# First token tiles one by one, and the value projection as TensorE's first work

## The chip, the cores and the metric

The kernel runs on one core of one Trainium2 chip. The metric is the time of one execution in device microseconds (us). Four runs of the kernel before gave 172.43 to 172.70 us, median 172.57 us. One execution was also recorded by the hardware profiler; "the trace" is its record, and times inside it count from the start of its span.

## The reference

For x of 2048 tokens by 448 features, in bf16:

```python
xn = layernorm(x)                                  # no weights, eps 1e-5
q, k, v = split(xn @ wqkv)                         # 16 heads of 28
# token s attends to s, s-2, ..., s-14 (8 keys, dilation 2), softmax over them
s = attention(q, k, v) @ wo
g = silu(gelu_tanh(xn @ w1 + b1) @ w2 + b2)        # 448 -> 1792 -> 448
out = x + s * g
```

## The kernel before

**Tokens.** Even and odd tokens are stored as two halves of 1024, so that a dilated window becomes 8 neighbours. There are 16 tiles of 128 tokens, in 4 chunks of 4 tiles. Attention is cut into blocks of 112 queries (128 at the start of a half), each of which needs 128 keys and values.

**Work of one chunk.** For each tile VectorE takes mean and variance (`stats`, L334: `bn_stats`, `bn_aggr`), ScalarE a square root and VectorE a reciprocal (`rstds`, L345), and VectorE writes the normalised tile (`norm`, L362). A row has 448 values; the 64 beyond 384 are written twice, so that the last part of the contraction can run in the upper or the lower half of TensorE's rows. In the first two chunks TensorE transposes the tile (L376) into a PSUM bank and ScalarE or VectorE copies it out into `xnT` (L380); in the last two a DMA transposes it. Then come the projections: query and key (`qk`, L417), value (`vproj`, L440), the first feed-forward matmul (`ff1`, L461, evacuated by a gelu on ScalarE with the bias `b1`), attention (`attn`), the second feed-forward matmul (`ff2`) and the output (`final`).

**Contractions in batches.** A contraction over 448 is three full matmuls of 128 rows and a tail of 64 rows. `batch` (L384) groups jobs: the closed jobs run their full matmuls first, then all tails run in pairs, one in each half of the array, then the opened jobs run their full matmuls. Each job holds one of 8 PSUM banks until ScalarE or VectorE has copied it out.

**Weights.** Query and key weights are loaded raw (`wraw`, and `wraw3` for the last 64 rows) and copied into a padded layout (`wqk`, `wqk3`, L320 to L329) by ScalarE or VectorE. Value weights (`wv`) and the feed-forward weights (`w1`, `w2`) are used as loaded.

**Who decides the order.** Each piece of work is a task with engines it may run on, an estimated cost, what it depends on, a priority and the buffers that it takes and gives. A list scheduler (`_Plan.run`, L73) goes through them and fixes one order for each engine's queue; the tasks are then written out in that order (L691). On the chip each engine works through its queue strictly in that order. So a changed cost or priority can move work anywhere in the kernel, and an instruction whose data is ready still waits behind an earlier one of its engine. Loads are issued by SyncE (SP) or ScalarE's queue in that order too.

**The start.** Up to 40 dummy matmuls on zeros (L272, "warm", while the plan's clock is under 12) keep TensorE busy until there is work. Tiles 0 and 1 are loaded from SP, 2 and 3 from ScalarE's queue (L313), then the raw query and key weights from SP. The square roots of tiles 0 and 1 are one instruction, those of 2 and 3 another (L603). All later loads except that of `b1` wait for the statistics of tile 0 (`t_hold`, L607, a small memset on VectorE); the value weights are issued from ScalarE's queue after the first square root (L608). The bias `b1` comes in as 14 rows, is transposed by TensorE (L626) and copied out by VectorE (L630, the tile is called `b` in the profile); every gelu needs it.

Of the kernel before, what the change touches and what calls it, by code (L numbers as in the profile page):

```python
# [10 lines left out]
ALU = mybir.AluOpType  # L11
ACT = mybir.ActivationFunctionType
# [131 lines left out]
def kernel(  # L144
# [12 lines left out]
    nc = tc.nc  # L157
    P = 128
    S, D, H, DH, F = A_x.shape[1], 448, 16, 28, 1792
# [5 lines left out]
    KF = 3 * P  # L165
# [3 lines left out]
    TPC = CH // P  # L169
# [15 lines left out]
    def rows(halves, pos, n):  # L185
        h, r = divmod(pos, HALF)
        return halves[h, r:r + n, :]
# [4 lines left out]
    def sb(name, shape, dt=BF16):  # L192
        return const.tile(shape, dt, name=name)
# [3 lines left out]
    x_sb = sb("x_sb", [P, NT, D])  # L197
# [4 lines left out]
    wv = sb("wv", [P, KT, D])  # L202
    w1 = sb("w1", [P, KT, F])
    w2 = sb("w2", [P, NMT, D])
    wo = sb("wo", [P, KT, D])
    b1r = sb("b1r", [NMT, P])
    b1 = sb("b1", [P, NMT], F32)
    b2 = sb("b2", [P, D])
# [9 lines left out]
    mv = sb("mv", [P, NT, 2], F32)  # L218
    sd = sb("sd", [P, NT], F32)
    rstd = sb("rstd", [P, NT], F32)  # L220

    def ring(name, n, shape, dt=BF16, fifo=False):
        return _Pool([sb(f"{name}{i}", shape, dt) for i in range(n)], fifo)

    p_xn = ring("xn", 6, [P, 512])
    p_st = ring("st", 4, [P, 6], F32)
# [14 lines left out]
    plan = _Plan()  # L241
# [7 lines left out]
    def act(n):  # L249
        return 0.19 + n / 1200.0  # L250

    def dve(n, r=1):
        return 0.15 + n / (960.0 * r)
# [10 lines left out]
    def memset(eng, ap, v):  # L264
        def fn(_):
            getattr(nc, eng).memset(ap, v)  # L266
        return fn
# [11 lines left out]
    def mk_ident(_):  # L279
# [5 lines left out]
    t_wz = [plan.add("DVE", 0.3, memset("vector", wqk[:, :, :, DH:], 0.0), [t_on], prio=98),  # L285
            plan.add("DVE", 0.1, memset("vector", wqk3[:, :, DH:], 0.0), [t_on], prio=97)]
# [3 lines left out]
    def dma(eng, dst, src, kb, prio, deps=()):  # L290
        def fn(_):
            (nc.sync if eng == "SP" else nc.scalar).dma_start(dst, src)  # L292
        a = plan.add(eng, 0.45, fn, [t_on] + list(deps), prio)
        return plan.add("DMA", kb / 310.0, lambda _: None, [a], prio, tail=1.7)
# [7 lines left out]
    t_x = {}  # L302

    def load_x(t0, n, prio, eng="SP", deps=()):
        d = dma(eng, x_sb[:, t0:t0 + n, :],
                rows(x_half, t0 * P, n * P).rearrange("(t p) d -> p t d", p=P), 112 * n, prio, deps)
        for t in range(t0, t0 + n):
            t_x[t] = d

    def ktiles(ap):  # L310
        return ap.rearrange("(k p) c -> p k c", p=P)

    for t in range(TPC):  # L313
        load_x(t, 1, 99 - t, "SP" if t < 2 else "ACT")
    t_raw = dma("SP", wraw[:], ktiles(A_wqkv[0:KF, 0:2 * D]), 672, 97)
    t_raw3 = [dma("SP", wraw3[64 * i:64 * i + 64, :], A_wqkv[KF:D, i * D:(i + 1) * D], 56, 96)
              for i in range(2)]


    t_wqk = []  # L320
    for kt in range(3):
        def fn(k, kt=kt):
            o, i = wqk[:, kt, :, :DH], wraw[:, kt, :].rearrange("p (h c) -> p h c", c=DH)
            copy(k.on, o, i)
        t_wqk.append(plan.add(("ACT", "DVE"), (act(2 * D), 0.45), fn, [t_raw] + t_wz, 95 - kt))

    def fn(k):
        copy(k.on, wqk3[:, :, :DH], wraw3[:].rearrange("p (h c) -> p h c", c=DH))
    t_wqk.append(plan.add(("ACT", "DVE"), (act(D), 0.3), fn, t_raw3 + t_wz, 91))  # L329


    t_st = {}

    def stats(t):  # L334
        def fn(k):
            s = buf(p_st, k)
            nc.vector.bn_stats(out=s[:], in_=x_sb[:, t, :])  # L337
            nc.vector.bn_aggr(out=mv[:, t, :], in_=s[:])
        k = plan.add("DVE", 0.75, fn, [t_x[t]], prio=98 - 3 * t if t < TPC else 70 - t, take=(p_st,))
        k.give = ((p_st, k, 0),)  # L340
        t_st[t] = k

    t_rs = {}

    def rstds(t0, n, gate=()):  # L345
        def f1(_):
            nc.scalar.activation(sd[:, t0:t0 + n], mv[:, t0:t0 + n, 1], ACT.Sqrt, bias=eps_t[:])

        def f2(_):
            nc.vector.reciprocal(rstd[:, t0:t0 + n], sd[:, t0:t0 + n])  # L350
        a = plan.add("ACT", 0.3, f1, [t_st[t] for t in range(t0, t0 + n)] + [t_eps] + list(gate), prio=95, table=("sqrt",))
        b = plan.add("DVE", 0.16, f2, [a], prio=95)
        for t in range(t0, t0 + n):
            t_rs[t] = b
        return a
# [6 lines left out]
    def norm(t, prio):  # L362
        def f1(k):
            xn = buf(p_xn, k)
            for o, i in ((xn[:, :D], x_sb[:, t, :]), (xn[:, D:], x_sb[:, t, KF:])):
                nc.vector.tensor_scalar(o, i, mv[:, t, 0:1], rstd[:, t:t + 1], op0=ALU.subtract, op1=ALU.mult)

        a = plan.add("DVE", 0.45, f1, [t_rs[t]], prio, take=(p_xn,))
        if t >= 2 * TPC:
            t_xT[t] = dma_T(xnT[:, :, t * P:(t + 1) * P], lambda: buf(p_xn, a)[:], [a], (p_xn, a, 0))  # L370
            return

        def f2(k):
            xn, tp = buf(p_xn, a), half_bank(buf(p_b, k))
            for kt in range(KT):
                nc.tensor.transpose(tp[:, kt, :], xn[:, kt * P:(kt + 1) * P], ident[:])  # L376
        b = plan.add("PE", 0.25, f2, [a, t_ident], prio, take=(p_b,), give=((p_xn, a, 0),), tail=0.15)

        def f3(k):
            copy(k.on, xnT[:, :, t * P:(t + 1) * P], half_bank(buf(p_b, b)))  # L380
        t_xT[t] = plan.add(("DVE", "ACT"), (dve(512, 2), act(512)), f3, [b], prio, give=((p_b, b, 0),))
# [58 lines left out]
    def vproj(b, half, prio):  # L440
        k0 = BLK[b][2]
        r = slice(64 * half, 64 * half + 64)

        def full(ps, kt, start, stop):
            nc.tensor.matmul(ps[:, :D], xnT[:, kt, k0:k0 + P], wv[:, kt, :], start=start, stop=stop)  # L445

        def tail(ps, start, stop):
            nc.tensor.matmul(ps[:, :D], xnT[r, 3, k0:k0 + P], wv[r, 3, :], start=start, stop=stop)  # L448

        def evac(a, own, i):  # L450
            def fn(k):
                copy(k.on, buf(p_v, own, i)[:, :, :DH], buf(p_b, own, i)[:, :D].rearrange("p (h c) -> p h c", h=H))
            t_v[b] = plan.add(("ACT", "DVE"), (act(D), dve(D)), fn, [a] + t_vw, prio + 2, give=((p_b, own, i),))
            v_at[b] = (p_v, own, i)
        return _Job(D, full, tail, half,
                    [t_xT[t] for t in range(k0 // P, (k0 + P - 1) // P + 1)] + t_wv, evac, (p_v,))
# [143 lines left out]

    for t in range(TPC):
        stats(t)
    t_sq = rstds(0, 2)  # L603
    rstds(2, 2)


    t_hold = plan.add("DVE", 0.07, memset("vector", x_sb[:1, 4, :1], 0.0), [t_st[0]], 96)  # L607
    t_wv = [dma("ACT", wv[:, 0:3, :], ktiles(A_wqkv[0:KF, 2 * D:]), 336, 95, [t_sq])]  # L608
    t_wv += [dma("ACT", wv[64 * i:64 * i + 64, 3, :], A_wqkv[KF:D, 2 * D:], 56, 94, [t_sq]) for i in range(2)]
    load_x(4, 4, 91, "SP", [t_hold])  # L610
    t_w1 = [dma("SP", w1[:, 0:3, :], ktiles(B_w1[0:KF, :]), 1344, 90, [t_hold])]
    t_w1 += [dma("SP", w1[64 * i:64 * i + 64, 3, :], B_w1[KF:D, :], 224, 89 - i, [t_hold]) for i in range(2)]
    t_b1r = dma("SP", b1r[:], B_b1.rearrange("(m f) -> m f", f=P), 4, 95)
    load_x(8, 4, 86, "SP", [t_hold])
    load_x(12, 4, 85, "SP", [t_hold])
    t_w2 = [dma("SP", w2[:], B_w2.rearrange("(m p) c -> p m c", p=P), 1568, 82, [t_hold])]
    t_b2 = dma("SP", b2[:], B_b2.rearrange("(o d) -> o d", o=1).to_broadcast((P, D)), 112, 81, [t_hold])
    t_wo = [dma("SP", wo[:, 0:3, :], ktiles(A_wo[0:KF, :]), 336, 80, [t_hold]),
             dma("SP", wo[:64, 3, :], A_wo[KF:D, :], 56, 79, [t_hold])]

    for t in range(TPC, NT):
        stats(t)
# [4 lines left out]
    a = plan.add("PE", 0.3, f1, [t_b1r, t_ident], 60, take=(p_b,), tail=0.15)  # L627
# [20 lines left out]
    blocks_of = [[b for b, (q0, nq, _) in enumerate(BLK) if (q0 + nq - 1) // CH == c] for c in range(NCH)]  # L648
    gate = [early]

    def project(c):
        p = (80, 79, 62, 58)[c]
        for t in range(c * TPC, (c + 1) * TPC):
            norm(t, 97 - 2 * t if t < TPC else p + 1)
        for t0, t1 in ((0, 2), (2, 4)) if c == 0 else ((c * TPC, (c + 1) * TPC),):
            for g in (0, 2):
                batch(*[[qk(t0, t1, h, w, p) for w in range(2)] for h in (g, g + 1)], p)
        vs = [vproj(b, i % 2, p) for i, b in enumerate(blocks_of[c])]
        batch(vs[:2], vs[2:], p - 0.1)

    project(0)
    t_os = [plan.add("POOL", 0.6, memset("gpsimd", o[:], 0.0), [t_xT[3]]) for o in p_os.bufs]
# [2 lines left out]
    for c, what in ((0, "F"), (0, "A"), (1, "A"), (1, "F"), (2, "A"), (2, "F"), (3, "A"), (3, "F")):  # L665
# [6 lines left out]
        else:  # L672
            p = 85 - c
# [48 lines left out]
```

## Time and profile before

| | |
|---|---|
| median of 4 runs | 172.57 us (172.43 to 172.70) |
| time of the profiled execution | 172.68 us |
| its span in the trace | 171.0 us |
| granted TensorE clock, mean | 0.999 |
| TensorE (PE) busy | 164.0 us, 96% of the span |
| VectorE (DVE) busy | 106.3 us, 62% |
| ScalarE (ACT) busy | 111.1 us, 65% |
| GpSimd (POOL) busy | 4.9 us, 3% |
| moved by DMA | 12.27 MB |

How to read the views. The page's strip of 40 slices (4.3 us each) shows each engine's busy share in tenths. The list of waits says who sat idle for whom: microseconds in total, number of times, longest. The chain that ended last is followed back from the last instruction; each line is start, length, and what took the time. The timeline lists instructions in order of time, neighbours of one kind merged: start, length, engine, line, operation, output from input, count, and in brackets the idle time before it and what ended it. "PEld" is the loading of weights into TensorE, which runs ahead of the matmul; "SPq" and "ACTq" are queues that issue DMAs. `L474` is line 474 of the kernel. Matmul ends are modelled, so the starts of weight loads are the better clock of TensorE's progress.

### The profile page before, as it was taken

What the parts mean: (1) busy time and instruction counts of PE and PEld (TensorE: products, weight loads), DVE (VectorE), ACT (ScalarE), POOL (GpSimd) and SP (SyncE); (2) the same over time, 40 slices, a digit from 0 to 9 for tenths busy, and PEclk for the clock granted to TensorE, in tenths of its full rate; (3) what the DMA queues carried; (4) which work ended last, traced back from release to release, by engine and by line L of the source; (5) the groups of instructions that cost most, each with busy time, mean ns of one, the idle gap of its engine ahead of it and who ended that gap; (6) DMA issues with size and microseconds to landing.
All of it is one profiled execution on the core that took longest, in us unless ns stands there. A gap on an engine that the chain in (4) does not pass through costs nothing.

```text
span 171.0 us, 3520 instructions
## 1 busy us (share of the span) xinstructions
PE 164.0 (96%) x1377; PEld 79.8 (47%) x1377; DVE 106.3 (62%) x290; ACT 111.1 (65%) x202; POOL 4.9 (3%) x18
## 2 busy tenths in 40 slices
PE   7999979999999999999999999999999999999990
PEld 2466343445455544434444553444655534455540
DVE  5699974189988899600196681013989951175663
ACT  3166199978788668787696678779655695911120
POOL 7300000000000000000000000000000000000000
PEclk9999999999999999999999999999999999999999
DMA  4999960033452122110001112000023220001101
GB/s 151 299 381 232 366 228 0 4 76 73 95 61 58 35 56 53 27 27 0 4 27 31 31 27 56 0 4 27 0 58 82 54 58 0 0 27 54 33 27 54
DMA packets 21741, 12.27 MB, mean 72 GB/s; under 512 B 13724, under 2 KB 21212, under 8 KB 21724
## 3 DMA queue, kind: packets, MB, share of 16 engines
q1 hardware_dynamic: 20876, 11.35, 25.1%
q10 hardware_dynamic: 848, 0.69, 1.5%
q8 instruction: 11, 0.18, 0.5%
q14 instruction: 6, 0.05, 0.1%
HBM read 7.06 MB, written 1.84 MB: 52 GB/s over the span
## 4 chain that ended last, share of the span: by engine, by line
PE 83%; DMA 9%; DVE 3%; SPq 1%; ACT 1%; issue 1%; DVEq 0%; ACTq 0%
PE bank L493 25%; PE bank L467 20%; PE bank L425 9%; PE bank L584 7%; PE bank L445 6%; DMA x_sb<-in_A_x_dram 6%; PE bank L557 5%; PE bank L470 4%; DMA wraw<-in_A_wqkv_dram 3%; PE bank L536 3%; PE bank L428 2%; SPq L292 1%; PE bank L448 1%; DVE st L337 1%; ACT L474 1%
## 5 line engine op out<-in xcount | busy, mean ns | idle before, releaser
L493 PE MATMUL bank<-w,h 128*128 128x448 bf16 x224 | 46.3, 352 | 0.0
L542 ACT ACTIVATE E<-bank 128x448 bf16<-128x448 f32 (+1 forms) x72 | 33.8, 558 | 9.3 <-PE bank L536 9.2
L467 PE MATMUL bank<-xnT,w 128*128 128x512 bf16 x168 | 39.1, 380 | 0.0
L474 ACT ACTIVATE h<-bank,b 128x512 bf16<-128x512 f32 x56 | 34.4, 693 | 4.7 <-PE bank L470 4.7
L509 DVE TENSOR_TENSOR y<-bank,b 128x448 f32<-128x448 f32 x16 | 9.9, 621 | 33.8 <-PE bank L493 33.8
L493 PEld LDWEIGHTS <-h 128*128 128x128 bf16 x224 | 21.1, 98 | 19.0
L467 PEld LDWEIGHTS <-w 128*128 128x128 bf16 x168 | 15.2, 97 | 21.1 <-issue 5.1
L425 PE MATMUL bank<-xnT,wqk 128*128 128x512 bf16 (+1 forms) x120 | 24.7, 337 | 0.0
L550 DVE TENSOR_TENSOR E<-E,m_gen 128x448 bf16<-128x448 bf16 x64 | 22.2, 385 | 1.3 <-ACT E L542 1.0
L515 ACT ACTIVATE t<-y 128x448 f32<-128x448 f32 x16 | 9.2, 577 | 17.5 <-DVE y L509 17.5
L557 PEld LDWEIGHTS <-E 128*128 128x128 bf16 x288 | 12.3, 96 | 9.5 <-DVE E L550 2.8
L589 DVE SCALAR_TENSOR_TENSOR sg<-bank,g 128x448 bf16<-128x448 f32 x16 | 10.0, 622 | 8.8 <-PE bank L584 7.9
L584 PE MATMUL bank<-wo,oT 128*128 128x448 bf16 x64 | 14.6, 353 | 0.1
L557 PE MATMUL bank<-v,E 128*128 128x29 bf16 x288 | 13.7, 176 | 0.0
L425 PEld LDWEIGHTS <-wqk 128*128 128x128 bf16 x120 | 10.2, 97 | 7.5 <-issue 1.7
L445 PE MATMUL bank<-wv,xnT 128*128 128x448 bf16 x54 | 12.3, 353 | 0.0
L569 DVE TENSOR_TENSOR os<-bank,rd 112x448 bf16<-112x448 f32 (+1 forms) x18 | 11.2, 624 | 1.0
L259 ACT CAST qT<-bank 128x512 bf16<-128x512 f32 (+1 forms) x15 | 7.9, 524 | 4.6 <-PE bank L428 2.4
L259 ACT CAST v<-bank 128x448 bf16<-128x448 f32 x13 | 6.9, 536 | 5.5 <-PE bank L445 3.7
L337 DVE BATCH_NORM_STATS2 st<-x_sb 128x6 f32<-128x448 bf16 x16 | 9.7, 608 | 1.1 <-DMA x_sb<-in_A_x_dram 1.0
L519 DVE SCALAR_TENSOR_TENSOR g<-t,y 128x448 bf16<-128x448 f32 x16 | 9.9, 618 | 0.2
L274 PE MATMUL bank<-warm 128*128 128x512 bf16 x24 | 8.4, 514 | 1.2 <-DVE warm L266 1.2
(53 smaller groups left out, 118.1 us busy)
## 6 DMA issues: line engine op xcount, KB each, us to landing
out_dram<-o SPq DMA_DIRECT2D x16, 112.0 KB, 1.7
w<-in_B_w_dram SPq DMA_DIRECT2D x1, 1568.0 KB, 8.9
x_sb<-in_A_x_dram SPq DMA_DIRECT2D x3, 448.0 KB, 7.7
w<-in_B_w_dram SPq DMA_DIRECT2D x1, 1344.0 KB, 10.8
wraw<-in_A_wqkv_dram SPq DMA_DIRECT2D x1, 672.0 KB, 6.0
w<-in_B_w_dram SPq DMA_DIRECT2D x2, 224.0 KB, 9.0
wv<-in_A_wqkv_dram ACTq DMA_DIRECT2D x1, 336.0 KB, 10.3
wo<-in_A_wo_dram SPq DMA_DIRECT2D x1, 336.0 KB, 6.3
```

Of the source, the lines that this page charges most:

```text
L259: nc.scalar.copy(o, i)
L337: nc.vector.bn_stats(out=s[:], in_=x_sb[:, t, :])
L425: nc.tensor.matmul(ps[:, :n], wqk[:, kt, hs, :], xnT[:, kt, cs], start=start, stop=stop)
L445: nc.tensor.matmul(ps[:, :D], xnT[:, kt, k0:k0 + P], wv[:, kt, :], start=start, stop=stop)
L467: nc.tensor.matmul(ps[:], w1[:, kt, ms], xnT[:, kt, cs], start=start, stop=stop)
L474: nc.scalar.activation(buf(p_h, own, i)[:], buf(p_b, own, i)[:], ACT.Gelu_apprx_tanh, bias=b1[:, mt:mt + 1])
L493: nc.tensor.matmul(ps[:, :D], buf(*h_at[(c, mt)])[:, j * P:(j + 1) * P], w2[:, mt, :], start=(mt == 0), stop=(mt == NMT - 1))
L542: nc.scalar.activation(buf(p_E, k)[:, :, :nq], buf(p_b, a, hl)[:, :4 * nq].rearrange("p (g q) -> p g q", g=4), ACT.Exp, scale=SCALE)
L550: nc.vector.tensor_tensor(out=E[:, :, :nq], in0=E[:, :, :nq], in1=m[:, :, :nq], op=ALU.mult)
L557: nc.tensor.matmul(ps[:, h, :DH + 1], buf(p_E, e)[:, g, :], buf(*v_at[b])[:, h, :DH + 1], start=True, stop=True)
L569: nc.vector.tensor_tensor(out=buf(p_os, k)[:nq, :D].rearrange("p (h c) -> p h c", h=H), in0=buf(p_b, po)[:nq, :].rearrange("p (h c) -> p h ...
L584: nc.tensor.matmul(ps[:, :D], oT[:, kt, t * P:(t + 1) * P], wo[:, kt, :], start=(kt == 0), stop=(kt == KT - 1))
```

## The change

- Tile 0 is loaded from SP and tile 1 from ScalarE's queue; then SP issues the value weights, the raw query and key weights, and tiles 2 and 3, in that order.
- `t_hold` is gone, and so is the value weights' wait for the first square root: all loads of the kernel but tile 1 are issued from SP without a condition, in the order of their priorities.
- The square roots and reciprocals of the first four tiles are four single ones instead of two pairs.
- The second copy of the last 64 columns of a normalised tile is a plain copy of the first instead of a second subtract and multiply.
- In chunk 0 the value blocks form two batches of one closed and one opened job each, planned ahead of the query and key jobs, the first with priority 96. The other chunks keep one batch after query and key.
- The planner's costs and priorities of the copies into `wqk`, of `stats` and of `norm` are changed.

```diff
-    for t in range(TPC):
-        load_x(t, 1, 99 - t, "SP" if t < 2 else "ACT")
+    load_x(0, 1, 99, "SP")
+    load_x(1, 1, 99, "ACT")
+    t_wv = [dma("SP", wv[:, 0:3, :], ktiles(A_wqkv[0:KF, 2 * D:]), 336, 98)]
+    t_wv += [dma("SP", wv[64 * i:64 * i + 64, 3, :], A_wqkv[KF:D, 2 * D:], 56, 98) for i in range(2)]
     t_raw = dma("SP", wraw[:], ktiles(A_wqkv[0:KF, 0:2 * D]), 672, 97)
     t_raw3 = [dma("SP", wraw3[64 * i:64 * i + 64, :], A_wqkv[KF:D, i * D:(i + 1) * D], 56, 96)
               for i in range(2)]
+    for t in range(2, TPC):
+        load_x(t, 1, 96, "SP")
...
-        t_wqk.append(plan.add(("ACT", "DVE"), (act(2 * D), 0.45), fn, [t_raw] + t_wz, 95 - kt))
+        t_wqk.append(plan.add(("ACT", "DVE"), (0.94, 0.39), fn, [t_raw] + t_wz, 96))
...
-    t_wqk.append(plan.add(("ACT", "DVE"), (act(D), 0.3), fn, t_raw3 + t_wz, 91))
+    t_wqk.append(plan.add(("ACT", "DVE"), (act(D), 0.3), fn, t_raw3 + t_wz, 96))
...
-        k = plan.add("DVE", 0.75, fn, [t_x[t]], prio=98 - 3 * t if t < TPC else 70 - t, take=(p_st,))
+        k = plan.add("DVE", 0.8, fn, [t_x[t]], prio=98 - 3 * t if t < TPC else 70 - t, take=(p_st,))
...
-            for o, i in ((xn[:, :D], x_sb[:, t, :]), (xn[:, D:], x_sb[:, t, KF:])):
-                nc.vector.tensor_scalar(o, i, mv[:, t, 0:1], rstd[:, t:t + 1], op0=ALU.subtract, op1=ALU.mult)
-
-        a = plan.add("DVE", 0.45, f1, [t_rs[t]], prio, take=(p_xn,))
+            nc.vector.tensor_scalar(xn[:, :D], x_sb[:, t, :], mv[:, t, 0:1], rstd[:, t:t + 1],
+                                    op0=ALU.subtract, op1=ALU.mult)
+            nc.vector.tensor_copy(xn[:, D:], xn[:, KF:D])
+
+        a = plan.add("DVE", 0.5, f1, [t_rs[t]], prio, take=(p_xn,))
...
-    t_sq = rstds(0, 2)
-    rstds(2, 2)
-
-
-    t_hold = plan.add("DVE", 0.07, memset("vector", x_sb[:1, 4, :1], 0.0), [t_st[0]], 96)
-    t_wv = [dma("ACT", wv[:, 0:3, :], ktiles(A_wqkv[0:KF, 2 * D:]), 336, 95, [t_sq])]
-    t_wv += [dma("ACT", wv[64 * i:64 * i + 64, 3, :], A_wqkv[KF:D, 2 * D:], 56, 94, [t_sq]) for i in range(2)]
-    load_x(4, 4, 91, "SP", [t_hold])
-    t_w1 = [dma("SP", w1[:, 0:3, :], ktiles(B_w1[0:KF, :]), 1344, 90, [t_hold])]
...
+    for t in range(TPC):
+        rstds(t, 1)
+
+
+    load_x(4, 4, 91, "SP")
+    t_w1 = [dma("SP", w1[:, 0:3, :], ktiles(B_w1[0:KF, :]), 1344, 90)]
...
+        vs = [vproj(b, i % 2, p) for i, b in enumerate(blocks_of[c])]
+        if c == 0:
+            for i in range(0, len(vs), 2):
+                batch(vs[i:i + 1], vs[i + 1:i + 2], 96 if i == 0 else p)
         for t0, t1 in ((0, 2), (2, 4)) if c == 0 else ((c * TPC, (c + 1) * TPC),):
             for g in (0, 2):
                 batch(*[[qk(t0, t1, h, w, p) for w in range(2)] for h in (g, g + 1)], p)
-        vs = [vproj(b, i % 2, p) for i, b in enumerate(blocks_of[c])]
-        batch(vs[:2], vs[2:], p - 0.1)
+        if c:
+            batch(vs[:2], vs[2:], p - 0.1)
```

The other loads (`w1`, `w2`, `b2`, `wo`, tiles 8 to 15) lose their `[t_hold]` in the same way.

More of the change, by code (lines that the diff above doesn't have):

```diff
@@ L602 @@
         stats(t)
-    t_sq = rstds(0, 2)
-    rstds(2, 2)
-    t_hold = plan.add("DVE", 0.07, memset("vector", x_sb[:1, 4, :1], 0.0), [t_st[0]], 96)
-    t_wv = [dma("ACT", wv[:, 0:3, :], ktiles(A_wqkv[0:KF, 2 * D:]), 336, 95, [t_sq])]
-    t_wv += [dma("ACT", wv[64 * i:64 * i + 64, 3, :], A_wqkv[KF:D, 2 * D:], 56, 94, [t_sq]) for i in range(2)]
-    load_x(4, 4, 91, "SP", [t_hold])
-    t_w1 = [dma("SP", w1[:, 0:3, :], ktiles(B_w1[0:KF, :]), 1344, 90, [t_hold])]
-    t_w1 += [dma("SP", w1[64 * i:64 * i + 64, 3, :], B_w1[KF:D, :], 224, 89 - i, [t_hold]) for i in range(2)]
-    t_b1r = dma("SP", b1r[:], B_b1.rearrange("(m f) -> m f", f=P), 4, 95)
[L614 to L619, printed above, removed]
+    for t in range(TPC):
+        rstds(t, 1)
+    load_x(4, 4, 91, "SP")
+    t_w1 = [dma("SP", w1[:, 0:3, :], ktiles(B_w1[0:KF, :]), 1344, 90)]
+    t_w1 += [dma("SP", w1[64 * i:64 * i + 64, 3, :], B_w1[KF:D, :], 224, 89 - i) for i in range(2)]
+    t_b1r = dma("SP", b1r[:], B_b1.rearrange("(m f) -> m f", f=P), 4, 95)
+    load_x(8, 4, 86, "SP")
+    load_x(12, 4, 85, "SP")
+    t_w2 = [dma("SP", w2[:], B_w2.rearrange("(m p) c -> p m c", p=P), 1568, 82)]
+    t_b2 = dma("SP", b2[:], B_b2.rearrange("(o d) -> o d", o=1).to_broadcast((P, D)), 112, 81)
+    t_wo = [dma("SP", wo[:, 0:3, :], ktiles(A_wo[0:KF, :]), 336, 80),
+             dma("SP", wo[:64, 3, :], A_wo[KF:D, :], 56, 79)]
     for t in range(TPC, NT):
```

## Prediction

> **What bounds the kernel now.** First the page and the list of waits: is TensorE ever idle, and for whom?
>
> ```profile
> PE   7999979999999999999999999999999999999990
> ```
>
> ```profile
> PE bank L274 <- DVE warm L266: 1.2, 1, 1.2
> PE bank L376 <- ACT h L474: 1.2, 2, 1.0
> ```
>
> ```profile
> ACT L474 <- DVE b L630: 3.7, 1, 3.7
> ```
>
> TensorE is full, apart from 1.2 us before the dummy matmuls and 1.2 us around 22 us, when all 8 PSUM banks are taken and it waits for the first gelus. So time can only be won before 24 us: by starting real work earlier, or by removing that stall. The third line says why the gelus were late: ScalarE waited 3.7 us for VectorE's copy of the bias. The chain shows what that copy waited for.
>
> ```profile
> 9.17 9.48 DMA x_sb<-in_A_x_dram
> 18.67 0.64 DVE st L337
> ...
> 20.97 0.07 DVE b L630
> 21.10 1.28 ACT L474
> 22.40 0.12 ACT h L474
> ...
> 24.32 0.54 PE bank L470 x4
> ...
> 31.01 1.14 PE bank L445 x6
> ```
>
> The bias copy is queued on VectorE behind the statistics of tiles 8, 9 and 10. Then follow a table load on ScalarE, the gelus, and at 24.32 TensorE's next tails; from there it runs without a gap through the end of the first feed-forward matmul at 31.01. Last, VectorE's timeline: is it the load at 18.65 that holds it, or its own queue?
>
> ```profile
> 16.94 1.62 DVE L366 TENSOR_SCALAR xn<-x_sb,mv,rstd 128x448 bf16<-128x448 bf16 x6
> 18.67 0.63 DVE L337 BATCH_NORM_STATS2 st<-x_sb 128x6 f32<-128x448 bf16 x1
> ```
>
> Both: VectorE was busy until 18.56, and the load came at the same moment. So the first gelu hangs on how much work VectorE has in front of the bias copy.
>
> **The change, part by part.** I follow the order in which the changed program's instructions stand on each engine.
>
> *TensorE's start.*
>
> ```profile
> 6.75 0.96 PEld L274 LDWEIGHTS <-warm 128*128 128x128 bf16 x5 [0.25 <-issue]
> 7.83 0.42 PEld L376 LDWEIGHTS <-xn 128*128 128x128 bf16 x4
> 9.57 0.75 PEld L425 LDWEIGHTS <-wqk 128*128 128x128 bf16 x6
> ```
>
> Now 17 dummies instead of 19 stand ahead of the first transposes. Before 6.75 they come every 0.43 us, afterwards every 0.215, so two fewer put the first transposes at 7.83 − 0.43 = 7.40; tile 0's normalised rows are there (they ended near 6.3 before, and wait for one square root less now). Two transposes and two dummies later, at 7.40 + 4·0.10 + 0.05 + 4·0.10 + 0.2 = 8.45, the value blocks begin, against 9.57 for the first query/key matmul: 1.1 us earlier. Their weights are in time: 672 KB stand in the queue up to them, and at the 270 GB/s of the stretch from 2 to 4 us they are through before 7.
>
> *Query and key weights.* They come behind 448 KB of value weights instead of 224 KB of tiles 2 and 3: 224 KB more, 0.8 us at 270 to 306 GB/s, so they land near 8.5 instead of 7.7. Their copies (0.39 each on VectorE, 0.94 on ScalarE) end by 9.65. TensorE wants them only after the first two value blocks, 8.45 + 1.5 = 10.0, so this is hidden; if the load came a microsecond later still, half of that would show. ScalarE's three issues of the value weights (5.0 to 8.2) go and block nothing any more; the copy behind them began at 8.22 and may begin at 8.5 now. The removed memset is 0.06 us on VectorE.
>
> *Work moved forward.* The four value blocks cost 1.14 at 31.01 and, in the chain, 0.48 + 1.24 from 37.88: 2.86 us. They move ahead of the feed-forward matmul, where they cost 2.86 plus one more entry into the tails, about 0.1. TensorE would reach its last transposes before the gelu-bound tails at 8.45 + 12.5 (9.57 to 22.1 before) + 2.96 + 0.18 (bias transposes, now in this stretch) + 0.65 (two more groups of transposes) = 24.75.
>
> *VectorE's queue, the step that decides.* From the statistics of tile 2 on, the changed order has in front of the bias copy 9 statistics, 6 norms, 6 bank copies for query and key, 2 transposed tiles and 3 reciprocals; before, counted from 9.54, it had 8, 6, 5, 0 and 2. By start-to-start intervals of the trace: statistics 0.73, norm 0.515 (I take 0.50 for the new pair: the subtract-and-multiply's 0.393 plus a small copy like the bias copy's 0.14, somewhat overlapped; ends 0.42 and 0.58), bank copy 0.33, transposed tile 0.39, reciprocal 0.16 to 0.22.
> - before: 8·0.73 + 6·0.515 + 5·0.33 + 0.39 = 10.97, so 20.51 without waits; measured 20.89, so 0.38 of waits.
> - after: 9·0.73 + 6·0.50 + 6·0.33 + 2·0.39 + 0.54 = 12.87. The queue gets there at 7.40 + 0.63 (transposes done) + 0.82 (two transposed tiles) + 0.6 + 0.2 (wqk copies) = 9.65. That makes 22.5 without waits. Waits are for TensorE, which brings tile 2's transposes at about 12.7 and evacuations after that later than before; between 0.4 (as before) and 1.6 I take 1.0: the bias copy starts at **23.5**, 2.6 us later than before.
>
> Nothing that ends the DMA stream helps here: tiles 8 to 11 stand behind the same bytes as before and VectorE wants them only at about 21.3.
>
> *The sum.* TensorE's tails wait for the second gelu. Before, the second wait ended at 23.72, 2.83 after the bias copy's start; the sequence from the tails to the end of the feed-forward matmul took 31.01 − 24.32 = 6.69. The changed order has the same sequence there, so it ends at 23.5 + 2.83 + 6.69 = 33.0, with the 2.86 of value blocks done: the same state would have been reached before at 33.87. Gain **0.85 us**; in general 24.35 minus the start of the bias copy. TensorE arrives at 24.75 and stalls in all some 1.3 us, no less than now: three quarters of what the change could bring goes into that stall.
>
> *Behind it.* ScalarE has three copies, two table loads (1.28 each) and two more copies between the last gelu and the first exponential; laid out with the trace's durations, the first masked exponential is ready some 0.9 us before TensorE wants it, so I count nothing, and 0.5 for smaller stalls in the changed order as a bound. Number and kinds of matmuls are otherwise equal, the tail after the last `ff2` as well.
>
> The granted clock stayed 1.00 through the 1.03 us stall. The Trainium skill ("TensorE: Matmul & The Clock Gate", Part 1: The HAM clock gate) says that an idle window of about 3.4 us halves the clock, for as long as it then takes to warm up again; the expected stalls are shorter, but by that rule a stall that grew past 3.4 us would cost another 1.7 and turn the gain into a loss.
>
> **Rivals.**
> - *VectorE is not late.* If its waits vanish and the bias copy comes by 22.2, TensorE runs through: from 24.75, plus 0.32 of transposes and 6.69, to 31.76, a gain of 2.1: 170.6. For it: 22.5 without waits is near. Against: VectorE waited before too, and TensorE delivers later now.
> - *No difference.* Bias copy between 24.0 and 24.7, or it comes at 23.5 and 0.5 us is given back in the attention's order: 172.6.
> - *Slower: the tiles 2 and 3 come late.* They now stand on SP behind six weight loads, and SP's queue can block: before, its issue from 4.66 on took 4.46 us for three loads, held until the raw weights had landed. Should tiles 2 and 3 be issued only after a landing, at 8 to 8.5, they come at about 11 instead of 9.5 and VectorE, which goes strictly in order, starts its 12.87 us at 11: bias copy at 24.3 to 25.5 with waits of 0.4 to 1.6. It decides from 24.7 on; at 25.2 the time is 173.5. Against it: SP was held with 2.6 MB outstanding, and here only 1.2 MB stand before tile 2.
>
> **How the numbers follow.** The profiled execution was 172.68 (span 171.0), 0.11 above the median. 172.68 − 0.85 = 171.83: I say 171.8. The measurement can tell about 0.2% (0.35 us). Forecast, a gain of 0.35 to 1.5: 0.43. VectorE not late: 0.15. No difference: 0.22. Slower, by the late tiles or by stalls in the attention's new order: 0.20. The likeliest case's own range is 171.1 to 172.3; the range to 170.5 takes in the first rival, to 173.3 most of the last. Faster 0.58, same 0.22, slower 0.20.
>
> **What would show it.** In the changed profile: value weights first used near 8.5; the bias copy on VectorE at 23 to 24 and still the releaser of ScalarE's first gelu table load; a stall of TensorE of 1 to 2 us between 24 and 27; the end of the first feed-forward matmul near 33; no other wait of TensorE. A bias copy before 22 or after 25, tiles 2 and 3 landing after 10.5, or new waits of TensorE after 40 would make the prediction wrong.

## The result and the profile after

| | before | after |
|---|---|---|
| median | 172.66 us (63 runs) | 172.08 us (43 runs) |
| ratio, 95% interval | | 0.9971 [0.9960, 0.9982] |
| time of the profiled execution | 172.68 us | 172.32 us |
| its span | 171.0 us | 170.6 us |

The change wins 0.29%, which is 0.50 us (0.31 to 0.69); 0.85 was forecast. The profiled executions differ by 0.36. Ratios, here and below, are over the runs in the chip's faster state, so they differ a little from quotients of medians, and the few runs outside it, on one chip up to 566 us, are left out.

Each run also has a span, from its first to its last instruction. The change's spans average 170.08 us; those of the kernel before, over 58 runs beside the experiments, 170.96: 0.88 less. But the time outside the span averages 2.01 us with the change and 1.76 before, and it reaches 2.83 in a run of the change, where no run before is above 1.90. In the kernels below it averages 1.72 or 1.73 wherever the value weights are late or the dummies are 13, and 1.91 to 2.08 in the others that have the change. No experiment looked for the cause; it stays open.

First the page and the list of waits, as before: who is TensorE idle for? (Columns of a wait: microseconds in total, number of times, longest.)

```profile
PE   7999988999999999999999999999999999999990
```

```profile
ACT L479 <- DVE b L632: 4.4, 1, 4.4
```

```profile
PE bank L274 <- DVE warm L266: 1.3, 1, 1.3
PE bank L381 <- ACT h L479: 0.9, 1, 0.9
PE bank L381 <- DVE xnT L261: 0.4, 1, 0.4
```

The strip is still full. ScalarE's wait for the bias copy `b` has grown from 3.7 to 4.4 us. TensorE waits once for a gelu (0.9 us), where it waited twice (1.2), and once for a transposed tile that VectorE has to copy out (0.4): 1.3 us in all. The stall has not gone. The chain of the kernel after shows why; its columns are start, length, and what took the time.

```profile
17.57 0.42 DVE kT L261
...
23.78 0.18 DVE mv L342
24.10 1.28 ACT L479
25.39 0.70 ACT h L479
26.13 0.38 PE bank L381 x4
26.52 0.57 PE bank L475 x4
...
33.23 1.29 PE bank L430 x6
```

The figure is the same as before, only later: statistics, bias copy, table load, gelus, transposes, and TensorE's tails (L475) at 26.52 instead of 24.32. The first feed-forward matmul ends at 33.23, with the four value blocks already done. Before, it ended at 31.01 and the value blocks came on top (2.86): 33.87. Up to 17.57 the chain runs through TensorE, from the dummies on; there VectorE has waited for a result of TensorE, and from there its own queue is the chain. So when TensorE starts also moves the copy; the dummies below come back to that.

The timeline of the kernel after has the starts that the prediction named.

```profile
7.50 0.43 PEld L381 LDWEIGHTS <-xn 128*128 128x128 bf16 x4
7.90 0.94 ACT L259 COPY wqk<-wraw 128x896 bf16<-128x896 bf16 x1 [2.59 <-DMA wraw<-in_A_wqkv_dram]
8.61 0.30 PEld L450 LDWEIGHTS <-xnT 128*128 128x128 bf16 x3 [0.20 <-DVE xnT L261]
9.70 0.62 DVE L341 BATCH_NORM_STATS2 st<-x_sb 128x6 f32<-128x448 bf16 x1
9.98 0.72 PEld L430 LDWEIGHTS <-wqk 128*128 128x128 bf16 x6
...
23.88 0.14 DVE L632 CAST b<-bank 128x14 f32<-128x14 bf16 x1
```

TensorE begins its first projections at 8.61 instead of 9.57, but VectorE reaches a copy of 0.14 us, which every gelu needs, at 23.88 instead of 20.89.

### The profile page after: what moved, and what is told of

Read it like the earlier page. It is cut to its first block, busy times and chain, and to the rows that moved or that the text cites. A ratio compares the mean times of both kernels' runs of the same rounds, so it can differ in the third digit from the quotient of the medians.

```text
span 170.6 us, 3510 instructions
## 1 busy us (share of the span) xinstructions
PE 163.4 (96%) x1372; PEld 79.0 (46%) x1372; DVE 109.4 (64%) x298; ACT 108.0 (63%) x197; POOL 4.9 (3%) x18
## 4 chain that ended last, share of the span: by engine, by line
PE 91%; DVE 5%; ACT 1%; issue 1%; DVEq 0%; ACTq 0%
PE bank L498 25%; PE bank L472 20%; PE bank L430 12%; PE bank L589 7%; PE bank L450 6%; PE bank L562 4%; PE bank L274 4%; PE bank L475 4%; PE bank L541 3%; PE bank L433 2%; PE bank L453 1%; DVE st L341 1%; PE bank L381 1%; DVE xn L369 1%; ACT L479 1%
## 5 line engine op out<-in xcount | busy, mean ns | idle before, releaser
L430 PE MATMUL bank<-xnT,wqk 128*128 128x512 bf16 (+1 forms) x120 | 24.1, 337 | 0.0
L562 PEld LDWEIGHTS <-E 128*128 128x128 bf16 x288 | 12.7, 96 | 9.7 <-DVE E L555 2.0
L261 DVE CAST kT<-bank 128x256 bf16<-128x256 f32 (+1 forms) x9 | 4.8, 532 | 15.1 <-PE bank L430 10.8
L562 PE MATMUL bank<-v,E 128*128 128x29 bf16 x288 | 14.4, 176 | 0.0
L259 ACT CAST qT<-bank 128x256 bf16<-128x256 f32 (+1 forms) x13 | 6.1, 471 | 4.8 <-PE bank L433 3.3
```

Of the source, the lines that this page charges most:

```text
L259: nc.scalar.copy(o, i)
L430: nc.tensor.matmul(ps[:, :n], wqk[:, kt, hs, :], xnT[:, kt, cs], start=start, stop=stop)
L562: nc.tensor.matmul(ps[:, h, :DH + 1], buf(p_E, e)[:, g, :], buf(*v_at[b])[:, h, :DH + 1], start=True, stop=True)
```

## The experiments

**Theory.** The bias copy's place in VectorE's queue sets the end of the kernel; TensorE's earlier start is worth nothing as long as that copy is late. **First rival.** TensorE is full, so the earlier start itself is the gain, and the stall around 24 us is only where TensorE rests. **Second rival.** The loads decide: value weights ahead of the query and key weights on SP. All ratios are against the kernel before on the same chip; each kernel ran 6 to 12 times.

### The bias copy early, in the changed kernel

The copy moves in VectorE's queue to right ahead of the reciprocal of tiles 4 to 7; nothing else moves.

```diff
     plan.run()
+    plan.order.remove(t_b1)
+    plan.order.insert(plan.order.index(t_rs[4]), t_b1)
```

> The changed kernel; only the copy of the bias on VectorE is moved, from behind the statistics of tiles 8 to 10 to ahead of the reciprocal of tiles 4 to 7; the order of everything else is kept. Theory (the first gelu hangs on VectorE's queue, and with it TensorE's stall): bias copy near 19.5 instead of 23.88, gelu table load right behind it, the 0.92 us wait of TensorE for a gelu gone, the 0.36 us wait for a transposed tile stays; the first feed-forward matmul ends near 32.2 instead of 33.2 and the time falls by about 1.0 us against the changed kernel (ratio to the kernel before about 0.991). Rival (the early work was never worth more, the time is lost again in attention): the stall goes, the time changes by less than 0.3 us.

Measured: 170.73 us, ratio 0.9901 [0.9873, 0.9929]. Against the change as made (0.9971) that is 0.70% or 1.2 us more. In its timeline:

```profile
18.74 0.17 DVE L632 CAST b<-bank 128x14 f32<-128x14 bf16 x1
...
19.03 1.28 ACT L479 ACT_TABLE_LOAD   x1
```

and in its list of TensorE's waits:

```profile
PE bank L274 <- DVE warm L266: 1.3, 1, 1.3
PE bank L381 <- DVE xnT L261: 0.4, 1, 0.4
PE bank L589 <- DVE y L514: 0.2, 1, 0.2
```

ScalarE no longer waits for the copy (no releaser stands behind the table load), and TensorE's wait for a gelu is gone. The chain has the end of the first feed-forward matmul 1.79 us earlier than in the kernel after (33.23), and the last operation comes 1.78 earlier:

```profile
31.44 1.29 PE bank L430 x6
```

Of that, 0.68 goes with an earlier start (first transposes at 6.82 instead of 7.50); the other 1.1 us is the copy's. So the stall was no mere resting place: taken away, its time is won.

### The same two lines in the kernel before

```diff
     plan.run()
+    plan.order.remove(t_b1)
+    plan.order.insert(plan.order.index(t_rs[4]), t_b1)
```

> The kernel before; only the copy of the bias is moved ahead of the reciprocal of tiles 4 to 7, nothing of the change is in it. Theory: the stall of 1.23 us goes whole, since the first tails of the feed-forward matmul end near 18.8 and gelus can start there; time falls by 1.0 to 1.2 us (ratio 0.993), more than the change itself brought. Rival (TensorE's late start is the loss, the stall only its echo): less than 0.5 us.

Measured: 171.28 us, ratio 0.9921 [0.9904, 0.9938]: 1.4 us from two lines, without the change.

```profile
15.64 0.16 DVE L630 CAST b<-bank 128x14 f32<-128x14 bf16 x1
...
17.36 1.28 ACT L474 ACT_TABLE_LOAD   x1
```

The copy needs nothing of the work that it stood behind; its task had only been planned late. With the blocker gone from both kernels, the change is worth 0.9901 against 0.9921, some 0.2%, and the intervals overlap. The spans say more: 168.95 us on average with the change and 169.62 without, six runs each, 0.67 less. The two profiled executions, whose first transposes start at 6.82 and 6.89, end 0.86 us apart.

### The bias copy later

Two more statistics of tile 8, whose results nobody uses, right ahead of the copy. Nothing of the computation is left out.

```diff
+    junk = sb("junk", [P, 6], F32)
...
+        for _i in range(2):
+            nc.vector.bn_stats(out=junk[:], in_=x_sb[:, 8, :])
```

> The changed kernel with two more statistics of one tile (results unused) on VectorE directly ahead of the bias copy, unknown to the planner, so the order is kept. Theory: bias copy at 25.3 instead of 23.88, stall longer by 1.4 us, time longer by 1.4 us one for one (ratio to the kernel before about 1.005). Rival (the stall has slack behind it): less than 0.5 us longer.

Measured: 173.87 us, ratio 1.0049 [1.0015, 1.0083], that is 0.78% or 1.3 us above the change as made. The intervals allow 0.6 to 2.1, and the runs fall into two groups (172.45 to 173.28, and 174.46 to 175.23), so they show only that it is longer. The timeline is sharper; the two statistics are L635.

```profile
3.36 0.15 PEld L274 LDWEIGHTS <-warm 128*128 128x128 bf16 x1 [0.28 <-issue]
3.79 2.12 PEld L274 LDWEIGHTS <-warm 128*128 128x128 bf16 x10 [0.28 <-issue]
6.02 0.43 PEld L381 LDWEIGHTS <-xn 128*128 128x128 bf16 x4
...
22.83 1.25 DVE L635 BATCH_NORM_STATS2 junk<-x_sb 128x6 f32<-128x448 bf16 x2
24.00 0.15 DVE L636 CAST b<-bank 128x14 f32<-128x14 bf16 x1
```

Without the two statistics the copy could have started at 22.83; it starts at 24.00, 1.17 us later. TensorE waits 2.3 us for it and its gelu, where the stall was 1.3 in the kernel after:

```profile
PE bank L381 <- ACT h L479: 1.3, 1, 1.3
PE bank L381 <- DVE b L636: 1.0, 1, 1.0
```

And the last operation starts 143.77 us behind the copy, as it does in the kernel after (143.76, table below). So an engine that is 64% busy passes all of the added 1.17 us on. Yet the copy is only 0.12 later than in the kernel after. The first transposes explain it: they came at 6.02 instead of 7.50. The order of work ahead of them is the same; what differs is the dummies' step, 0.43 us each until 3.8 here, and until 6.8 there:

```profile
6.35 0.15 PEld L274 LDWEIGHTS <-warm 128*128 128x128 bf16 x1 [0.28 <-issue]
6.78 0.60 PEld L274 LDWEIGHTS <-warm 128*128 128x128 bf16 x3 [0.28 <-issue]
```

(These two are of the kernel after.) So one profile against another can be off by 1.5 us at the start, and a kernel's runs are needed beside it. This execution was also the shortest of its 12.

### Value weights and value blocks late again

All of the change but the early value projection: the value weights go behind the first feed-forward weights on SP, and the value blocks of chunk 0 are one batch planned behind query and key, as before. They still run ahead of the first feed-forward matmul or between its parts; in the kernel before they ran behind it.

```diff
-    t_wv = [dma("SP", wv[:, 0:3, :], ..., 336, 98)]      # ahead of wraw
+    t_wv = [dma("SP", wv[:, 0:3, :], ..., 336, 88)]      # behind w1
...
-        if c == 0:
-            for i in range(0, len(vs), 2):
-                batch(vs[i:i + 1], vs[i + 1:i + 2], 96 if i == 0 else p)
...
-        if c:
-            batch(vs[:2], vs[2:], p - 0.1)
+        batch(vs[:2], vs[2:], p - 0.1)
```

> The changed kernel with the value weights loaded from SP behind the first feed-forward weights instead of ahead of the query and key weights, and its four value blocks in one batch planned after query and key: the first real work of TensorE is query and key again, near 9.6, with dummies until then, and the value blocks stand between query/key and the feed-forward matmul. Theory (the bias copy decides, not TensorE's start): bias copy between 22.5 and 24, time within 0.4 us of the changed kernel (172.1). Rival (the gain comes from the value blocks in TensorE's idle time): about 1 us slower than the changed kernel.

Measured: 172.26 us, ratio 0.9968 [0.9949, 0.9986]: the same as the change (0.9971). Its chain:

```profile
10.11 0.76 PE bank L428 x6
...
17.77 1.13 PE bank L448 x6
...
33.07 1.29 PE bank L428 x6
```

TensorE's first real work is a query/key block at 10.11; in the kernel after it is a value block, which the chain has at 8.75. That is 1.4 us later, and the first feed-forward matmul still ends at 33.07 against 33.23, because the stall of 1.3 us is not there. Its whole list of TensorE's waits:

```profile
PE bank L274 <- DVE warm L266: 1.2, 1, 1.2
PE bank L628 <- DMA b1r<-in_B_b_dram: 1.0, 1, 1.0
PE bank L587 <- DVE y L512: 0.2, 1, 0.2
```

So the early start alone bought the stall, and the first rival falls. The theory does not hold for this kernel either, though its copy is at 22.84 and ScalarE waits 2.4 us for it: TensorE waits for no gelu, so here TensorE's own work sets the end. That both kernels take the same time is partly a coincidence of two limits.

### Both: value blocks late, bias copy early

```diff
     # the edit before this one, and
+    plan.order.remove(t_b1)
+    plan.order.insert(plan.order.index(t_rs[4]), t_b1)
```

> The kernel with the late value weights, and the bias copy moved ahead of the reciprocal of tiles 4 to 7. With the wait for the gelu gone, what TensorE has done before 24 us should count at last. Theory: value blocks ahead of query and key put about 1 us of work into time that was dummies, so this one is 0.6 to 1.2 us slower than the changed kernel with the early bias copy (ratio to the kernel before 0.994 to 0.997 against 0.990). Rival (an early start of TensorE is worth nothing even then): equal, 0.990.

Measured: 171.59 us, ratio 0.9929 [0.9902, 0.9956]; with the value blocks first and the bias early it was 0.9901. The order favours the early start by 0.28%, about 0.5 us, but the intervals overlap. The spans average 169.85 us against 168.95, 0.9 longer, inside the forecast of 0.6 to 1.2: with the copy out of the way the early start counts, in part taken back by the time outside the span.

### Value weights from ScalarE's queue

Same order of work, but the value weights no longer stand ahead of the query and key weights on SP.

```diff
-    t_wv = [dma("SP", wv[:, 0:3, :], ...
-    t_wv += [dma("SP", wv[64 * i:64 * i + 64, 3, :], ...
+    t_wv = [dma("ACT", wv[:, 0:3, :], ...
+    t_wv += [dma("ACT", wv[64 * i:64 * i + 64, 3, :], ...
```

> The changed kernel with the value weights issued from ScalarE's queue right behind tile 1 instead of from SP; every engine's order of work is kept. Theory (both ways the value weights and the raw query and key weights are there before TensorE or VectorE wants them, the bytes are the same): raw weights land within 1 us of before, value blocks start when the transposes are done, bias copy within 0.4 us of 23.9, time within 0.3 us of the changed kernel (ratio to the kernel before 0.997). Rival (the order on one queue is what the change lives on): raw weights later, at least 0.5 us slower.

Measured: 171.84 us, ratio 0.9961 [0.9936, 0.9986]; the change as made lies inside. The raw weights were there 1.5 us earlier (7.90 in the kernel after):

```profile
6.42 0.94 ACT L259 COPY wqk<-wraw 128x896 bf16<-128x896 bf16 x1 [1.08 <-DMA wraw<-in_A_wqkv_dram]
```

No gain outside the intervals came of it. From the first transposes to the bias copy it is 16.39 us here (6.64 to 23.03) and 16.38 in the kernel after (7.50 to 23.88). The second rival falls for these starts of TensorE: the order of these loads is hidden.

### The norm as two subtract-and-multiplies again

```diff
-            nc.vector.tensor_scalar(xn[:, :D], x_sb[:, t, :], mv[:, t, 0:1], rstd[:, t:t + 1],
-                                    op0=ALU.subtract, op1=ALU.mult)
-            nc.vector.tensor_copy(xn[:, D:], xn[:, KF:D])
+            for o, i in ((xn[:, :D], x_sb[:, t, :]), (xn[:, D:], x_sb[:, t, KF:])):
+                nc.vector.tensor_scalar(o, i, mv[:, t, 0:1], rstd[:, t:t + 1], op0=ALU.subtract, op1=ALU.mult)
```

> The changed kernel with the last 64 columns of a normalised tile computed twice again, as before, instead of copied; the planner's costs and the orders are kept. Theory: 0.52 us a tile both ways (0.515 before, 0.52 in the changed kernel), bias copy within 0.2 us of 23.9, no difference (ratio 0.997). Rival (the copy is slower because it waits for the first write, or faster): six tiles stand ahead of the bias copy, so 0.1 us a tile would show as 0.6 us.

Measured: 171.82 us, ratio 0.9942 [0.9924, 0.9960]. In its timeline four norms last from 18.56 to 20.62:

```profile
18.56 2.14 DVE L370 TENSOR_SCALAR xn<-x_sb,mv,rstd 128x448 bf16<-128x448 bf16 x8
20.62 0.62 DVE L341 BATCH_NORM_STATS2 st<-x_sb 128x6 f32<-128x448 bf16 x1
```

and in the kernel after, from 19.60 to 21.68:

```profile
19.60 0.40 DVE L369 TENSOR_SCALAR xn<-x_sb,mv,rstd 128x448 bf16<-128x448 bf16 x1
...
21.68 0.62 DVE L341 BATCH_NORM_STATS2 st<-x_sb 128x6 f32<-128x448 bf16 x1
```

2.06 against 2.08 us: a pair costs 0.52 in either form, so the new form saves nothing. That the old form's runs came out 0.29% lower is not explained by this price. Its profiled copy (22.83) is earlier because the dummies' wide step ended earlier: from the first transposes (6.46) to the copy it is 16.37, in the kernel after (7.50) 16.38. The runs' granted clocks point the same way. All six of the old form have a mean of 0.995 to 0.999, and a median of 171.82; the change's runs at 0.995 to 0.999 have a median of 171.70, those at 1.000 one of 172.41. So the six runs are as long as the change's runs of the same clock, and the 0.29% fits chance in the step. (Why the clock tells them apart stands in the last section.)

### Fewer dummies

If the dummies' step moves the bias copy, fewer dummies ahead of the transposes should too.

```diff
-    for _ in range(40):
+    for _ in range(13):
```

In the changed kernel with the early bias copy:

> The changed kernel with the early bias copy and 13 dummy matmuls instead of 19. The number of dummies that ran at half speed was 15 in the profile of the changed kernel and 8 to 12 in the profiles of three other kernels with the same dummies, so the first transposes wait for the dummies. Theory: first transposes near 6.5 instead of 7.0 to 7.7, then VectorE and the query and key weights (landing near 7.9) set the pace; 0.2 to 0.8 us faster than the early bias copy alone (ratio to the kernel before 0.985 to 0.989). Rival (the clock then comes up later and the early matmuls run at half speed): equal or slower.

Measured: 170.44 us, ratio 0.9864 [0.9839, 0.9889], the lowest of all. In its profile the wide step lasted longer than the dummies: the first transposes start at 6.35, and the last operation comes only 0.05 us earlier than with all dummies (165.81 against 165.86). In the changed kernel alone:

> The changed kernel with 13 dummies instead of 19, the bias copy left where the change has it. In five profiles of the changed order the end came 144.15 us after the start of the bias copy, to 0.02 us, while the bias copy itself came between 22.8 and 24.0 with the number of dummies at half speed (10 to 15). Theory (the dummies delay the first transposes, those delay VectorE's queue, and that the bias copy): first transposes near 6.8 whatever the clock does, bias copy 22.8 to 23.1, end again 144.15 later; ratio to the kernel before 0.993 to 0.996, with a narrow spread. Rival (dummies only fill time): bias copy and time as in the changed kernel, ratio 0.997.

Measured: 171.48 us, ratio 0.9929 [0.9906, 0.9952], against 0.9971 for the change as made, 0.7 us more. Its first transposes and its bias copy:

```profile
5.95 0.42 PEld L381 LDWEIGHTS <-xn 128*128 128x128 bf16 x4
...
22.95 0.14 DVE L632 CAST b<-bank 128x14 f32<-128x14 bf16 x1
```

The transposes wait for the dummies in the kernel after (7.50), and 1.5 us earlier they bring the copy 0.93 earlier. Not all of the 1.5 us is the dummies': where the wide step ended as early as here (its last wide step begins at 5.07 in both), all dummies put the transposes at 6.82, in the kernel with the early copy. And the copy of 22.95 is no earlier than that of the norm as two (22.83, with transposes at 6.46), since TensorE now waits for VectorE's copy of the query and key weights, so that the order of the loads may matter again (no run tests it):

```profile
8.89 0.10 PEld L430 LDWEIGHTS <-wqk 128*128 128x128 bf16 x1 [0.52 <-DVE wqk L261]
```

The forecast had the transposes near 6.8; they came at 5.95. It also had a narrow spread, and the runs lie between 170.75 and 172.34 us. So the gain stands by the runs, whose intervals do not touch, but the profiles show only in part how it comes about: of the 0.6 us between the mean times, 0.3 is span (169.76 against 170.08) and 0.3 is time outside it. With the early bias copy the step is from 0.9901 to 0.9864, where the intervals still overlap. In the kernel before:

> The kernel before with 13 dummies instead of 24. Theory: there the bias copy waits for the load of tiles 8 to 11, which landed at 18.65, not for the dummies; bias copy within 0.3 us of 20.9, time within 0.4 us of the kernel before (ratio 0.998 to 1.002). Rival (the dummies delay this kernel as well): 0.5 to 1 us faster.

Measured: 173.66 us, ratio 1.0005 [0.9969, 1.0041]; its runs lie between 171.6 and 175.15 us. In its profile the copy starts at 20.53, 0.36 earlier than before, just outside the forecast of 0.3, and the last operation 0.36 earlier. The runs are inconclusive.

### The copy's start and the kernel's end

All starts are of the profiled executions: the copy and the last `final` on VectorE in the timelines, the end of the first feed-forward matmul of chunk 0 in the chains. The last two columns are differences to the last operation.

| kernel | bias copy | end of feed-forward | last operation | from copy | from feed-forward |
|---|---|---|---|---|---|
| after | 23.88 | 33.23 | 167.64 | 143.76 | 134.41 |
| bias copy later | 24.00 | 33.37 | 167.77 | 143.77 | 134.40 |
| value weights from ScalarE's queue | 23.03 | 32.37 | 166.78 | 143.75 | 134.41 |
| norm as two | 22.83 | 32.18 | 166.59 | 143.76 | 134.41 |
| 13 dummies | 22.95 | 32.29 | 166.70 | 143.75 | 134.41 |
| bias copy early | 18.74 | 31.44 | 165.86 | 147.12 | 134.42 |
| bias copy early, 13 dummies | 18.71 | 31.41 | 165.81 | 147.10 | 134.40 |
| value blocks late | 22.84 | 33.07 | 167.48 | 144.64 | 134.41 |
| value blocks late, bias copy early | 17.90 | 32.82 | 167.23 | 149.33 | 134.41 |
| before | 20.89 | 31.01 | 167.98 | 147.09 | 136.97 |
| before, 13 dummies | 20.53 | 30.65 | 167.62 | 147.09 | 136.97 |
| before, bias copy early | 15.64 | 29.77 | 166.72 | 151.08 | 136.95 |

```profile
167.64 0.39 DVE L599 TENSOR_TENSOR o<-x_sb,sg 128x448 bf16<-128x448 bf16 x1
```

(Kernel after; the lines of the other kernels look the same.) In the first five rows the end follows the copy to 0.02 us, over 1.2 us of the copy's start; in the two rows of the kernel before that have a late copy it does too. An earlier start of TensorE would move both as well, so the rows that move the copy alone decide: the later copy keeps the law, and the early one takes the stall away. At 18.74 the law no longer holds (162.5 would follow): there the copy is not what TensorE waits for, and with late value blocks it is not either.

The last column does not move at all: whatever happens ahead of it, 134.4 us follow the first feed-forward matmul in the changed kernels, and 137.0 in the kernel before, where they include the value blocks. So what these experiments move is won or lost wholly ahead of about 33 us.

## Why the prediction was right, and where a size was off

The mechanism and the sign were right, the place of the stall too; the gain was put too high, 0.85 against 0.50 in the runs and 0.36 between the profiles.

| step | predicted | measured |
|---|---|---|
| first transposes | 7.40 | 7.50 |
| value blocks begin | 8.45 | 8.61 |
| raw weights land | near 8.5 | 7.86 |
| VectorE reaches tile 2's statistics | 9.65 | 9.70 |
| first query/key matmul | 10.0 | 9.98 |
| norm pair | 0.50 | 0.52 |
| VectorE's waits up to the bias copy | 1.0 | 1.31 |
| bias copy | 23.5 | 23.88 |
| TensorE's stalls | some 1.3 | 0.92 for a gelu and 0.36 for a transposed tile |
| bias copy to the end of TensorE's last wait | 2.83 | 2.25 |
| from there to the tails | 0 (left out) | 0.39 |
| end of the feed-forward matmul | 33.0 | 33.23 |
| given back behind it | 0 (bound 0.5) | 0.30 |

- **VectorE's waits** are the first mis-sized term. The queue of 12.87 us began at 9.70, so a copy at 23.88 means 23.88 − 9.70 − 12.87 = 1.31 of waits, inside the bound of 0.4 to 1.6, but 0.31 above the value that I took. This is what the assumed prices leave over: the timeline names 0.8 us of idle time for TensorE in it, and 0.12 is the norm pairs (six at 0.52 instead of 0.50). The copy came 0.38 late.
- **From the copy to the tails** two errors nearly cancelled. The sum goes from the end of TensorE's wait straight to the tails and leaves out the transposes between them. Before, these took 24.32 − 23.72 = 0.60, so the same sum gives 20.89 + 2.83 + 6.69 = 30.41 for the kernel before, whose matmul ended at 31.01. After, they took 0.39. On the other side "TensorE's tails wait for the second gelu" did not hold: the list of waits has one wait for a gelu instead of two, and it ended 2.25 behind the copy, not 2.83. That 33.0 came within 0.2 of 33.23 is in part luck.
- **"I count nothing" behind 33 us** is the second. The gain at the end of the feed-forward matmul was 33.87 − 33.23 = 0.64, and the last operation came 167.98 − 167.64 = 0.34 earlier: 0.30 is given back. It belongs to the changed order and not to one execution, for the last column of the table above has 134.41 against 136.97 − 2.86 = 134.11. Late value blocks have it too. Summed from start to start, the matmuls of probabilities and values (L557, now L562) take 9.23 us instead of 8.64 behind 33 us; other lines take less (the scores, L536, now L541, 5.62 instead of 5.94), so this is only the largest of several differences. What they wait for there no list of waits names, and no run took it apart: this cause stays open.
- **The break-even.** The prediction had the gain as 24.35 minus the copy's start. The table above gives 20.89 + (147.09 − 143.76) = 24.22. That this is right to 0.13 is again two errors against each other: 0.17 won between the copy and 33.23, 0.30 lost behind it.
- **"VectorE is not late"**, priced at 170.6, was the rival that this order did not take; with the copy moved by hand the time is 170.73. The price was right, with the matmul's end at 31.44 instead of 31.76 in an execution that started 0.68 us earlier than the kernel after.
- **"Tiles 2 and 3 come late"** did not happen: SP issued them from 4.76 on, 3.6 us ahead of their landing near 8.4. **"No difference"** was the nearest rival: 0.12 more on the copy would have been its lower end.
- **The runs' gain (0.50) is above the profile's (0.36).** The prediction was worked out from a trace whose wide dummies lasted to 6.75, and in the profile after they lasted to 6.78. With like starts the change wins 0.36, less than half of the forecast. But two thirds of the change's runs have a mean granted clock below 1.000, the mark of an earlier start, and the spans win 0.88 on average; the time outside the span takes back 0.25. Neither was in the prediction, so part of the nearness of 0.50 to 0.85 is luck.

## What to carry to other kernels

When TensorE is full, look for the one small instruction that everything later needs, and at its place in a strictly ordered queue: here a copy of 0.14 us behind three statistics cost more than the whole change won, on an engine that was idle more than a third of the time. Before work is moved forward, count what it puts in front of that instruction; two added lines that move it were worth 1.4 us in the kernel before, and the change, without them, 0.5.

## What the runs showed of the hardware

**The dummies' step varies between executions.** Dummies of 128x512 came every 0.43 us at first and every 0.215 us later. The wide step ended at 3.8 us in one profile and at 6.8 in another of a program that is the same up to there, and it moved the first real work from 6.02 to 7.50. The granted clock of the profile's rows read 1.00 all the while and shows nothing of it at the start. It shows at the end: in the execution with the norm as two, whose wide step ended before 5 us, it reads 0.83 from 168 to 169 us and 0.50 from there on, inside the span and behind the last matmul; in the kernel after it stays 1.00. So a run's mean granted clock below 1 mostly goes with an early end of the wide step and, with the change, with a shorter run (171.70 against 172.41 us); the execution with the later bias copy, wide until 3.8 and at 1.00, is an exception. The Trainium skill ("TensorE: Matmul & The Clock Gate", Part 1: The HAM clock gate) states a clock window of about 3.4 us that runs freely, and start-to-start steps of 426.7 ns cold and 215.7 ns warm for 512 columns: the steps agree with 0.43 and 0.215. It gives ±500 ns for the spread of the transition, and this does not agree: here it was 3.0 us between two executions. It also says that one kernel had 6, 11 or 14 slow matmuls in different runs; that agrees, seven steps of 0.43 us being 3.0 us.

**Dummies can be in the way.** They keep TensorE busy in order, and while each takes 0.43 us the first transposes stand behind them: with 13 instead of up to 40 these started at 5.95 instead of 6.82 in two executions whose wide step ended alike, and the ratio went from 0.9971 to 0.9929.
